# Tying the first experts' matmul groups to turns of the attention on TensorE, and running the fourth block's four full units ahead of their tails

## The chip, the cores and the metric

The kernel runs on one core of one Trainium2 chip. The metric is the device time of one execution in microseconds (us). Before the change the median of 3 runs is 1228.98 us (1228.93 to 1230.21).

## The reference

Three stages follow each other, all in float32. An attention with a threshold (4 batches, 8 heads, 576 rows, head size 64) feeds a first pair of expert matmuls with a squared relu, and that feeds a second pair with a gate (`mish`):

```python
scores = (q @ k.T) / sqrt(64)
scores = where(scores >= max(scores) - tau, scores, -1e9)
attn = exp(scores - max(scores)); attn = attn / (sum(attn) + 1e-9)
x = (attn @ v)                      # to 2304 x 512
r = maximum(x @ w_in, 0); x = (s * r * r + b) @ w_out      # 512 -> 2048 -> 512
h = x @ w2_in; out = (h * tanh(softplus(h))) @ w2_out      # 512 -> 2048 -> 512
```

Float32 precision is reached with pairs of fp32r parts (a high and a low one), so one product takes three matmuls. The second pair is computed with fewer products on sums of quarters, whose weight parts must first be combined.

## The kernel before, in words

**Attention.** Heads go in 16 pairs (four pairs to a batch), and each pair takes nine *turns*; a turn is numbered k = 9 x pair + ti, from 0 to 143. A turn's `scores` (L324) multiplies on TensorE (PE) into the tile S (L340, 4 matmuls, 8 at ti = 4). VectorE (DVE) negates and takes the maximum into ns (L344), ScalarE (ACT) takes the exponential e (L351), DVE masks and sums it (L355), GpSimd (POOL) scales it (L365). From block 0 on S has one buffer (two banks of PSUM), so the next S waits for the L344 before it. Seven turns later (LAG) `weights_t` (L371) transposes a column of e on PE into T (L377 to L386), ACT copies it to te (L388), and a turn after that `product` (L391) multiplies with v into pv (L399). At a pair's last product `split_x` (L407) writes the pair's x with ACT and DVE (L412, L413) and stores a tail of 64 columns to DRAM. Twice in each pair `prep_qk` (L296) makes the next pair's q and k.

**First experts.** `moe1(b)` (L482) treats one batch, called a block: 32 *groups* of 12 matmuls each (`group`, L499, matmuls on L503), 16 into h (`layer1`) and 16 into y (`layer2`). It needs the block's four x, that is x of pair 4b + 3. Each unit's weights w are loaded by the SP queue (L496) into a ring of five slots (for block 0 they are split in place, L63 to L72). ACT makes relu, square and so on of h (L516 to L519), POOL subtracts (L520; DVE in block 3), DVE adds up y (L533). Block 3 runs after the attention, and has beside each full unit (512 columns) a *tail* unit of 256 columns from the tile xt, with the last 64 columns of all four batches.

**Combined weights.** `combine` (L88) makes the second experts' weight parts: raw loads crawi and crawo (L84), then ACT (L98), DVE (L99 to L111, L138), ACT (L136), and stores to wsi and wso (L140) on the SP queue. A step's result tiles share three slots, its intermediate tile has one. The first 12 of 16 steps must be done before the attention's pools are closed; the last four of those 12 are the tiles afo and chlo numbered 0 to 3. Only then is xt placed in that memory and loaded (L848, L849).

**The order.** The program is written by generators that take turns by a running count, attention with higher priority, and a scheduler sets each engine's order from the written order, the priorities and a model of time. Each engine, and the SP queue, then works its instructions off in that order:

```python
if a_on and (not m_on or (a_done - 5000.0) / a_left <= m_done / m_left):
    with tc.high_priority(offset=200):
        c = next(att, None)
else:
    c = next(mo, None)
```

Block 3 takes its units in the order of the list ORDER (L879): part 0 of layer 1 (two full units, two tails), part 1 (two full units, two tails), and so on.

Of the kernel before, what the change touches and what calls it, by code (L numbers as in the profile page):

```python
# [19 lines left out]
class Fused:  # L20
    def __init__(self, tc, q, k, v, tau, w_in, w_out, s, b, w2_in, w2_out, out):
        self.tc, self.nc = tc, tc.nc
        self.q, self.k, self.v, self.tau = q, k, v, tau
        self.s, self.b, self.out = s, b, out
        self.w_in, self.w_out, self.w2_in, self.w2_out = (w.bitcast(I32) for w in (w_in, w_out, w2_in, w2_out))
        self.B, self.H, self.S, self.D = q.shape
        self.NP = self.H // 2
        self.x, self.w1, self.w1s, self.wf, self.g, self.yc, self.ycd, self.es, self.raws = {}, {}, {}, {}, {}, {}, {}, {}, {}
        self.nd = self.n_s = self.n_acc = self.combined = 0
        self.m3 = self.hl = None  # L30


    def consts(self, pool):
# [290 lines left out]
    def scores(self, pr, ti):  # L324
        nc = self.nc
        Q, KH, KL, E4 = self.sets[pr % 2]
        if ti == 0:
            self.st = self.at.tile([P, 5, 9], F32, tag="stat", name=f"st{pr}", bufs=2)
        st = self.st
        nm, nthr, sm, u, rinv = (st[:, i, :] for i in range(5))  # L330
        hs = [0] if ti < 4 else [1] if ti > 4 else [0, 1]
        cols = slice(512, 640) if ti == 4 else slice((ti % 5) * 128, (ti % 5) * 128 + 128)
        S = self.s_tile(f"S{pr}_{ti}")
        for hf in range(2):
            ks = slice(hf * 288, hf * 288 + 288)
            so = S[:, hf * HB:hf * HB + 288]
            terms = [(h, K[h]) for h in hs for K in (KH, KL)]
            for i, (h, kt) in enumerate(terms):
                c0 = ti * 128 + 64 * h if ti <= 4 else 64 + ti * 128
                nc.tensor.matmul(so, Q[:, c0:c0 + 128], kt[:, ks], start=(i == 0), stop=(i == len(terms) - 1))  # L340
        ns = self.at.tile([P, 576], F32, tag="ns", name=f"ns{pr}_{ti}", bufs=2)
        sv = S.rearrange("p (h n) -> p h n", h=2)[:, :, :288]
        c1 = slice(ti, ti + 1)
        nc.vector.tensor_scalar(ns.rearrange("p (h n) -> p h n", h=2), sv, -0.125, 3.0e38,  # L344
                                op0=ALU.mult, op1=ALU.min, accum_out=nm[:, c1])
        nc.vector.tensor_scalar(nthr[:, c1], nm[:, c1], self.tau_c, None, op0=ALU.add)

        if ti < 4:
            self.es[pr, ti, "pair"] = self.at.tile([P, 1152], F32, tag="e", name=f"e{pr}_{ti}", bufs=8)
        e = E4[:, 64:640] if ti == 4 else self.es[pr, ti % 5, "pair"][:, 0 if ti < 4 else 576:][:, :576]  # L350
        nc.scalar.activation(e, ns, AF.Exp, bias=nm[:, c1], scale=-1.0)  # L351
        self.es[pr, ti] = e

        def finish():
            nc.vector.scalar_tensor_tensor(e, ns, nthr[:, c1], e, op0=ALU.is_le, op1=ALU.mult, accum_out=sm[:, c1])  # L355
            if ti not in (1, 4, 8):
                return
            g = slice({1: 0, 4: 2, 8: 5}[ti], ti + 1)
            nc.vector.tensor_scalar(rinv[:, g], sm[:, g], 1.0e-9, None, op0=ALU.add)
            nc.vector.reciprocal(rinv[:, g], rinv[:, g])  # L360

            nc.vector.tensor_scalar(u[:, g], sm[:, g], 0.5, 1.0 / self.S, op0=ALU.is_lt, op1=ALU.mult)
            for j in range(g.start, g.stop):
                t = self.es[pr, j]
                nc.gpsimd.tensor_scalar(t, t, rinv[:, j:j + 1], u[:, j:j + 1], op0=ALU.mult, op1=ALU.add)  # L365

        return finish
# [3 lines left out]
    def weights_t(self, pr, ci):  # L371
        nc = self.nc
        T = self.tp.tile([P, 1024], F32, tag="T", name=f"T{pr}_{ci}")
        E4 = self.sets[pr % 2][3]
        o = ci * 128
        for i in range(4):
            nc.tensor.transpose(T[:, i * 128:i * 128 + 128], self.es[pr, i, "pair"][:, o:o + 128], self.ident)  # L377
        if ci != 4:
            h = 0 if ci < 4 else 1

            c0 = 64 + o - 576 * h
            nc.tensor.transpose(T[:, 512:640], E4[:, c0:c0 + 128], (self.ident, self.swap)[h])  # L382
        else:

            nc.tensor.matmul(T[:, 512:576], E4[:, 0:128], self.ident[:, HALVES[1]], start=True, stop=False)
            nc.tensor.matmul(T[:, 512:576], E4[:, 576:704], self.ident[:, HALVES[0]], start=False, stop=True)  # L386
        te = self.at.tile([P, 576], F32, tag="te", name=f"te{pr}_{ci}", bufs=6)
        nc.scalar.copy(te, T[:, :576])  # L388
        return te

    def product(self, pr, c, tes, first, last):  # L391
# [28 lines left out]
    def attention(self):  # L420
# [2 lines left out]

        nc = self.nc
        N = 9 * self.B * self.NP
        LAG = 7
        for n in "kq":
            self.load_raw(0, n)
        nc.sync.dma_start(self.tau_c, self.tau.partition_broadcast(P))
# [9 lines left out]
        for k in range(N + LAG + 2):  # L439
            pr, ti = divmod(k, 9)  # L440
# [15 lines left out]
            if 0 <= j < N:  # L456
                prj, ci = divmod(j, 9)
                tnew = self.weights_t(prj, ci)
                yield 550
            if todo:  # L460
                tp, tc, te = todo
                tes[tc] = te
                if tc == 4:
                    self.product(tp, 4, (te, te), True, False)
                    yield 490
                elif tc > 4:
                    self.product(tp, tc - 5, (tes[tc - 5], te), False, tc == 8)
                    yield 970
                if tc == 8:
                    self.split_x(tp)  # L470
                    self.load_raw(tp + 2, "v")
            todo = (prj, ci, tnew) if 0 <= j < N else None


# [6 lines left out]

    def moe1(self, b):  # L482

        nc = self.nc
        full = "", [(self.x[4 * b + p][:, 0, :512], self.x[4 * b + p][:, 1, :512]) for p in range(4)], self.gp, 512, b
        runs = [full + (dict(),)]
        if b == 3:
# [10 lines left out]

        def group(acc, w, rhs, n):  # L499
            i = 0  # L500
            for c in range(4):
                for wl, xl in ((0, 0), (0, 1), (1, 0)):
                    nc.tensor.matmul(acc[:, :n], w[:, wl, c], rhs[c][xl], start=(i == 0), stop=(i == 11))  # L503
                    i += 1
                    if i in ((3, 6, 9) if n == 512 else (6,)):
                        yield 680

        def layer1(qf, part):
            ws = {fc: unit(0, qf, fc) for fc in (2 * part, 2 * part + 1)}
            for s, xs, pool, n, _, gs in runs:  # L510
                for fc, w in ws.items():
                    gh, gl = gs[qf, fc] = [pool.tile([P, n], F32R, tag=t, name=f"{t}{s}{b}_{qf}_{fc}", bufs=5 if s else 6) for t in ("gh", "gl")]
                    acc = self.acc(f"h{s}{b}_{qf}_{fc}")
# [21 lines left out]
                    if qf == 3:  # L535
                        nc.sync.dma_start(self.yd[dst, e // 2][:, e % 2], ye)

        for layer, qf, part in ORDER:
            yield from (layer1, layer2)[layer](qf, part)


    def y_combos(self, sb, direct):
# [326 lines left out]


EARLY = 12
HALVES = [slice(0, 64), slice(64, 128)]

N2 = 384
# [48 lines left out]
```

## Time and profile before

| what | value |
|---|---|
| median of 3 runs | 1228.98 us |
| the profiled execution | 1232.59 us, of which the span is 1230.7 us |
| PE matmul busy / weight load (PEld) | 93% / 78% of the span |
| DVE, ACT, POOL busy | 64%, 52%, 20% |
| mean granted TensorE clock | 0.96 |

The profile shows one execution. Times count from the span's start; "<-" after an idle time names what ended it; SPq is the DMA-issuing queue of SP. The clock is given as a share of full speed; it has two levels, 1 (2.4 GHz) and 0.5 (1.2 GHz). On DVE each turn shows two records at L344, the pass over S and a read of its accumulator.

### The profile page before, as it was taken

To read this page: it belongs to the slowest core of one execution; us is meant where nothing else is said; L and a number is where in the kernel's file an instruction comes from. 1 tells how busy PE (TensorE), PEld (TensorE's weight loads), DVE (VectorE), ACT (ScalarE), POOL (GpSimd) and SP (SyncE) were. 2 spreads that over 40 slices of the span, in tenths; PEclk is the share of its full clock that TensorE was granted. 3 is DMA by queue.
4 is the path that set the end of the run, shared out by engine and by line. 5 is a ranking of instruction groups with operands and counts; after the bars stand their busy time and mean duration, and the time that the engine had idled before them with its cause. 6 is when DMAs were issued, how large, how long until landed. Compare 5 with 4: busy or idle time off the path is not lost.

```text
span 1230.7 us, 18932 instructions
## 1 busy us (share of the span) xinstructions
PE 1139.8 (93%) x6796; PEld 956.4 (78%) x6796; DVE 784.9 (64%) x1682; ACT 642.5 (52%) x1061; POOL 243.0 (20%) x234
## 2 busy tenths in 40 slices
PE   7997999989999999899996729999999999999998
PEld 6765766666768777587875318888999999999998
DVE  6978684778724576765548753573479456934683
ACT  4665867464666554586644537763345234523351
POOL 3443432224232221342312200320000000000000
PEclk9998999889999999799997769999999999999999
DMA  6576466556874868678654665894799899998774
GB/s 149 118 184 187 111 218 207 179 180 210 274 209 148 261 227 230 200 247 241 226 153 178 227 232 161 335 384 157 273 357 384 322 392 362 358 328 295 272 252 144
DMA packets 145966, 294.39 MB, mean 239 GB/s; under 512 B 55184, under 2 KB 83344, under 8 KB 137552
## 3 DMA queue, kind: packets, MB, share of 16 engines
q1 hardware_dynamic: 138640, 288.75, 70.4%
q10 hardware_dynamic: 7232, 4.43, 1.4%
q8 instruction: 54, 0.88, 0.3%
q14 instruction: 40, 0.33, 0.1%
HBM read 202.64 MB, written 67.37 MB: 219 GB/s over the span
## 4 chain that ended last, share of the span: by engine, by line
PE 77%; DVE 8%; DMA 5%; issue 3%; POOL 3%; ACT 2%; SPq 1%; ACTq 0%; DVEq 0%; POOLq 0%
PE o L727 14%; PE h L503 13%; PE y L503 12%; PE pv L399 7%; PE qY L593 6%; PE S L340 5%; PE qV L593 4%; PE qX L593 4%; PE T L377 4%; POOL e L365 3%; PE yt L503 2%; PE ht L503 2%; DVE e L355 2%; DVE ns L344 1%; PE T L382 1%
## 5 line engine op out<-in xcount | busy, mean ns | idle before, releaser
L365 POOL TENSOR_SCALAR e<-e,st 128x576 f32<-128x576 f32 x128 | 135.7, 1072 | 245.4 <-DVE st L360 202.3
L727 PE MATMUL o<-wo,hl 128*128 128x256 f32 x1512 | 179.6, 279 | 0.0
L727 PEld LDWEIGHTS o<-wo,hl 128*128 128x128 f32 x1512 | 179.2, 188 | 0.0
L344 DVE TENSOR_SCALAR_CACHE_REDUCE ns<-S 128x576 f32<-128x576 f32 x144 | 107.9, 753 | 102.8 <-PE S L340 101.2
L503 PE MATMUL h<-x,w 128*128 128x512 f32 x576 | 145.8, 402 | 2.7 <-DVE x L413 2.7
L388 ACT COPY te<-T 128x576 f32<-128x576 f32 x144 | 91.7, 637 | 99.4 <-PE T L382 86.6
L377 PE MATMUL T<-ident,e 128*128 128x128 f32 x576 | 107.6, 291 | 30.8 <-ACT te L388 15.8
L355 DVE SCALAR_TENSOR_TENSOR e<-ns,st,e 128x576 f32<-128x576 f32 x128 | 113.2, 889 | 27.1 <-ACT e L351 25.9
L351 ACT ACTIVATE e<-ns,st 128x576 f32<-128x576 f32 x128 | 98.8, 777 | 60.5 <-DVE ns L344 55.0
L503 PEld LDWEIGHTS h<-x,w 128*128 128x128 f32 x576 | 107.5, 192 | 28.9 <-DVE x L413 3.2
L503 PE MATMUL y<-gh,w 128*128 128x512 f32 x384 | 126.3, 397 | 0.6 <-ACT gh L519 0.5
L340 PE MATMUL S<-KH,Q 128*128 128x288 f32 x320 | 101.9, 334 | 23.9 <-DVE ns L344 20.0
L377 PEld LDWEIGHTS T<-ident,e 128*128 128x128 f32 x576 | 73.1, 147 | 64.9 <-ACT te L388 23.8
L399 PE MATMUL pv<-te,rawv 128*64 128x288 f32 x640 | 122.6, 429 | 0.0
L520 POOL TENSOR_TENSOR gl<-r,gh 128x512 fp32r<-128x512 f32 x48 | 65.0, 1356 | 209.6 <-ACT gh L519 169.4
L340 PEld LDWEIGHTS S<-KH,Q 128*128 128x128 f32 x320 | 64.0, 200 | 44.1 <-DVE ns L344 27.0
L340 PE MATMUL S<-KL,Q 128*128 128x288 f32 x320 | 93.1, 306 | 0.0
L593 PE MATMUL qY<-yc,wi 128*128 128x384 f32 x432 | 87.6, 338 | 1.9 <-DVE g L616 1.9
L503 PEld LDWEIGHTS y<-gh,w 128*128 128x128 f32 x384 | 71.8, 188 | 19.3 <-issue 2.2
L593 PEld LDWEIGHTS qY<-yc,wi 128*128 128x128 f32 x432 | 76.3, 187 | 2.9 <-DVE g L616 2.9
L503 PE MATMUL y<-gl,w 128*128 128x512 f32 x192 | 76.3, 398 | 0.0
L645 DVE TENSOR_TENSOR hl<-g,hl 128x768 fp32r<-128x768 f32 x60 | 56.4, 954 | 20.8 <-ACT hl L709 20.7
(152 smaller groups left out, 2013.2 us busy)
## 6 DMA issues: line engine op xcount, KB each, us to landing
w<-w SPq DMA_DIRECT2D x96, 512.0 KB, 4.6
wo<-wso SPq DMA_DIRECT2D x42, 1024.0 KB, 7.2
wi<-wsi SPq DMA_DIRECT2D x23, 1024.0 KB, 8.1
wi<-wsi SPq DMA_DIRECT2D x25, 768.0 KB, 7.6
w<-wp SPq DMA_DIRECT2D x32, 512.0 KB, 3.4
wsi<-chli SPq DMA_DIRECT2D x24, 512.0 KB, 4.3
wso<-chlo SPq DMA_DIRECT2D x24, 512.0 KB, 5.4
ycd<-yp SPq DMA_DIRECT2D x14, 768.0 KB, 8.4
```

The source lines that it names most:

```text
L340: nc.tensor.matmul(so, Q[:, c0:c0 + 128], kt[:, ks], start=(i == 0), stop=(i == len(terms) - 1))
L344: nc.vector.tensor_scalar(ns.rearrange("p (h n) -> p h n", h=2), sv, -0.125, 3.0e38, op0=ALU.mult, op1=ALU.min, accum_out=nm[:, c1])
L351: nc.scalar.activation(e, ns, AF.Exp, bias=nm[:, c1], scale=-1.0)
L355: nc.vector.scalar_tensor_tensor(e, ns, nthr[:, c1], e, op0=ALU.is_le, op1=ALU.mult, accum_out=sm[:, c1])
L365: nc.gpsimd.tensor_scalar(t, t, rinv[:, j:j + 1], u[:, j:j + 1], op0=ALU.mult, op1=ALU.add)
L377: nc.tensor.transpose(T[:, i * 128:i * 128 + 128], self.es[pr, i, "pair"][:, o:o + 128], self.ident)
L388: nc.scalar.copy(te, T[:, :576])
L399: return self.nc.tensor.matmul(self.pv[HALVES[h], hf * HB:hf * HB + 288], v[:, h, c, :], tes[h][:, hf * 288:hf * 288 + 288], start=first, ...
L503: nc.tensor.matmul(acc[:, :n], w[:, wl, c], rhs[c][xl], start=(i == 0), stop=(i == 11))
L520: (nc.vector if b == 3 else nc.gpsimd).tensor_tensor(gl, r, gh.bitcast(F32), op=ALU.subtract)
L593: self.nc.tensor.matmul(acc, a, b, start=(first and i == 0), stop=(i == n - 1), skip_group_check=True)
L727: nc.tensor.matmul(bank[p][t], hl[:, gl, j, ts], w[:, 2 * (q % 2) + j, wl], start=(old is None and q + j + k == 0), stop=(q + j + k == 6), ...
```

## The change

Each turn of the attention keeps the last PE instruction of its scores (from turn 144 on, of its transposes) in a list `turns`. In blocks 0 to 2 the first and the seventh matmul of each group of 12 are queued on PE behind one of these turns: group g (1 to 96 over the three blocks) and half i/12 behind turn 44 + int((g - 1 + i/12) x 36/32), at most the last one. Eight groups so take nine turns, which is 32 groups to four pairs. The link only sets PE's order; it adds no semaphore wait. In block 3 both parts of the first layer-1 entry run as one: four full units, then their four tails.

```diff
+                self.turn = nc.tensor.matmul(so, Q[:, c0:c0 + 128], kt[:, ks], start=(i == 0), stop=(i == len(terms) - 1))
...
+        if 9 * pr + ci + LAG >= 9 * self.B * self.NP:
+            self.turn = turn
...
+            self.turns.append(self.turn.ins)
             todo = (prj, ci, tnew) if 0 <= j < N else None
...
         def group(acc, w, rhs, n):
             i = 0
+            self.groups += 1
             for c in range(4):
                 for wl, xl in ((0, 0), (0, 1), (1, 0)):
-                    nc.tensor.matmul(acc[:, :n], w[:, wl, c], rhs[c][xl], start=(i == 0), stop=(i == 11))
+                    if b < 3 and i % 6 == 0:
+                        turn = self.turns[min(FIRST + int((self.groups - 1 + i / 12) * 36 / 32), len(self.turns) - 1)]
+                        with tc.issue_after(turn):
+                            nc.tensor.matmul(acc[:, :n], w[:, wl, c], rhs[c][xl], start=(i == 0), stop=(i == 11))
+                    else:
+                        nc.tensor.matmul(acc[:, :n], w[:, wl, c], rhs[c][xl], start=(i == 0), stop=(i == 11))
...
-        def layer1(qf, part):
-            ws = {fc: unit(0, qf, fc) for fc in (2 * part, 2 * part + 1)}
-            for s, xs, pool, n, _, gs in runs:
+        def layer1(qf, *parts):
+            held = {}
+            for (s, xs, pool, n, _, gs), part in [(r, p) for r in runs for p in parts]:
+                if not s:
+                    held[part] = {fc: unit(0, qf, fc) for fc in (2 * part, 2 * part + 1)}
+                ws = held[part]
...
-        for layer, qf, part in ORDER:
-            yield from (layer1, layer2)[layer](qf, part)
+        order = ORDER if b < 3 else [(0, 0, 0, 1)] + ORDER[2:]
+        for layer, *key in order:
+            yield from (layer1, layer2)[layer](*key)
...
+LAG = 7
+FIRST = 44
```

The built programs show where the instructions went. In the listings a row is one instruction or a run of equal ones; the line numbers of the changed program are its own.

First place: PE at turns 134 to 136 (the tile S of pair 14's turn 8 and pair 15's turns 0 and 1; T are transposes; h and y are groups of the first experts). Before:

```order
L340 MATMUL S_8_5880<-KH_126,Q_123 128x288
L340 MATMUL S_8_5880<-KL_128,Q_123 128x288
L340 MATMUL S_8_5880<-KH_126,Q_123 128x288
L340 MATMUL S_8_5880<-KL_128,Q_123 128x288
L340 MATMUL S_0_5912<-KH_133,Q_131 128x288
L340 MATMUL S_0_5912<-KL_135,Q_131 128x288
L340 MATMUL S_0_5912<-KH_133,Q_131 128x288
L340 MATMUL S_0_5912<-KL_135,Q_131 128x288
L340 MATMUL S_1_5957<-KH_133,Q_131 128x288
L340 MATMUL S_1_5957<-KL_135,Q_131 128x288
L340 MATMUL S_1_5957<-KH_133,Q_131 128x288
L340 MATMUL S_1_5957<-KL_135,Q_131 128x288
```

The changed program, about turn 136:

```order
L513 MATMUL y_1_3_6506<-gl_1_3_6239,w_1_1_3_6482 128x512
L513 MATMUL y_1_3_6506<-gh_1_3_6238,w_1_1_3_6482 128x512
L341 MATMUL S_1_5957<-KH_133,Q_131 128x288
L341 MATMUL S_1_5957<-KL_135,Q_131 128x288
L341 MATMUL S_1_5957<-KH_133,Q_131 128x288
L341 MATMUL S_1_5957<-KL_135,Q_131 128x288
L511 MATMUL h_2_2_6529<-x_3671,w_0_2_2_6523 128x512
L513 MATMUL h_2_2_6529<-x_3671,w_0_2_2_6523 128x512 x2
L513 MATMUL h_2_2_6529<-x_4113,w_0_2_2_6523 128x512 x3
L511 MATMUL h_2_2_6529<-x_4552,w_0_2_2_6523 128x512
L513 MATMUL h_2_2_6529<-x_4552,w_0_2_2_6523 128x512 x2
L513 MATMUL h_2_2_6529<-x_4999,w_0_2_2_6523 128x512 x3
```

Three S stood directly behind one another; now a whole group of 12 matmuls of block 2 stands between two of them. Counted over the program, the matmuls of blocks 0 to 2 up to S of turn 84 go from 428 to 417, from there up to S of turn 143 from 724 to 639, and behind it from 0 to 96. Turns with none of them, from turn 45 on, were 49, 51, 59 to 62, 69 to 71, 105 to 113 and 133 to 142; in the changed program they are 60, 61 and 68 to 71.

Second place: the SP queue, at the end of the attention (crawo are raw loads of a combination step, chlo its results, w loads into the ring: w_0_0_1 to w_0_0_3 are block 3's first units, yd stores of block 2's results). Before:

```order
L84 DMA crawo_6556<-in_moe_w_out_dram 128x1024
L84 DMA crawo_6558<-in_moe_w_out_dram 128x1024
L140 DMA wso<-chlo_6612 128x512
L140 DMA wso<-chlo_6560 128x2x512
L140 DMA wso<-chlo_6561 128x2x512
L84 DMA crawo_7041<-in_moe_w_out_dram 128x1024
L84 DMA crawo_7043<-in_moe_w_out_dram 128x1024
L140 DMA wso<-chlo_6625 128x2x512
L84 DMA crawo_6693<-in_moe_w_out_dram 128x1024
L84 DMA crawo_6695<-in_moe_w_out_dram 128x1024
L140 DMA wso<-chlo_6697 128x2x512
```

The changed program:

```order
L500 DMA w_0_0_1_6921<-w_0_0_1_1411 128x1024
L141 DMA wso<-chlo_6561 128x2x512
L549 DMA yd_0_61<-y_0_5598 128x512
L549 DMA yd_0_61<-y_1_5599 128x512
L500 DMA w_0_0_2_6965<-w_0_0_2_1593 128x1024
L141 DMA wso<-chlo_6625 128x2x512
L500 DMA w_0_0_3_6967<-w_0_0_3_1670 128x1024
L85 DMA crawo_6693<-in_moe_w_out_dram 128x1024
L549 DMA yd_1_62<-y_2_5600 128x512
L85 DMA crawo_6695<-in_moe_w_out_dram 128x1024
```

Loads into the ring and stores of block 2's results, which stood well ahead of these steps before, now stand between the steps' own loads and stores.

Third place: PE in block 3 (h full units, ht tails). Before:

```order
L503 MATMUL h_0_1_6946<-x_5416,w_0_0_1_6921 128x512 x3
L503 MATMUL h_0_1_6946<-x_5874,w_0_0_1_6921 128x512 x3
L503 MATMUL h_0_1_6946<-x_6258,w_0_0_1_6921 128x512 x3
L503 MATMUL h_0_1_6946<-x_6477,w_0_0_1_6921 128x512 x3
L503 MATMUL ht_0_0_6967<-xt,w_0_0_0_6919 128x256 x3
L503 MATMUL ht_0_1_6988<-xt,w_0_0_1_6921 128x256 x3
L503 MATMUL h_0_2_7013<-x_5416,w_0_0_2_7007 128x512 x3
```

The changed program:

```order
L513 MATMUL h_0_3_6992<-x_5416,w_0_0_3_6967 128x512 x3
L513 MATMUL h_0_3_6992<-x_5874,w_0_0_3_6967 128x512 x3
L513 MATMUL h_0_3_6992<-x_6258,w_0_0_3_6967 128x512 x3
L513 MATMUL h_0_3_6992<-x_6477,w_0_0_3_6967 128x512 x3
L513 MATMUL ht_0_0_7013<-xt,w_0_0_0_6919 128x256 x3
L513 MATMUL ht_0_1_7038<-xt,w_0_0_1_6921 128x256 x3
```

Two full units (24 matmuls) stood ahead of the first one that reads xt, now four do (48).

## Rows read from the trace of the kernel before

**Rows 1.** The page: the span, and its first part on TensorE.

```profile
span 1230.7 us, 18932 instructions
PE 1139.8 (93%) x6796; PEld 956.4 (78%) x6796; DVE 784.9 (64%) x1682; ACT 642.5 (52%) x1061; POOL 243.0 (20%) x234
```

**Rows 2.** Busy time by stretch: stretch, its length, each engine, PE clock, DMA share, GB/s.

```profile
122.90:348.10 225.20, 209.49 (x1071) 152.63 (x1072) 158.97 (x381) 141.57 (x231) 72.18 (x61) 0.96 0.64 200
348.10:681.70 333.60, 313.60 (x1657) 238.43 (x1655) 201.23 (x499) 189.67 (x305) 95.06 (x87) 0.95 0.67 207
681.70:738.00 56.30, 26.51 (x107) 15.09 (x107) 34.92 (x72) 24.61 (x44) 3.96 (x4) 0.69 0.68 239
```

**Rows 3.** The same stretches, L344 on DVE alone (two records to a turn).

```profile
122.90:348.10 225.20, 30.45 (x80) 0.96 0.64 200
348.10:681.70 333.60, 44.95 (x118) 0.95 0.67 207
```

**Rows 4.** The same stretches, the first experts' matmuls (L503) on PE and PEld.

```profile
122.90:348.10 225.20, 115.87 (x429) 79.63 (x430) 0.96 0.64 200
348.10:681.70 333.60, 181.22 (x724) 131.49 (x723) 0.95 0.67 207
```

**Rows 5.** The chain of waits: start, us, what; runs of matmuls.

```profile
752.08 5.44 PE h L503 x24
...
605.93 0.53 PE S L340 x4
...
610.97 0.44 PE T L377 x4
611.51 1.12 PE pv L399 x8
```

**Rows 6.** Two stretches of nine turns each: L344 on DVE, then L503 on PE, PEld.

```profile
391.60:454.00 62.40, 6.86 (x18) 1.00 0.73 224
535.30:600.80 65.50, 6.86 (x18) 1.00 0.80 253
...
391.60:454.00 62.40, 47.25 (x191) 34.46 (x190) 1.00 0.73 224
535.30:600.80 65.50, 46.70 (x193) 35.15 (x192) 1.00 0.80 253
```

**Rows 7.** Busy time by stretch, where next to no L503 stands.

```profile
487.40:521.80 34.40, 27.86 (x152) 19.39 (x151) 27.26 (x77) 17.99 (x29) 9.44 (x9) 0.80 0.69 203
...
207.30:218.70 11.40, 7.17 (x46) 4.98 (x44) 9.95 (x27) 9.12 (x16) 1.28 (x1) 0.98 0.69 219
261.00:273.40 12.40, 7.76 (x35) 6.25 (x34) 9.69 (x26) 9.01 (x15) 1.27 (x1) 0.72 0.91 278
```

**Rows 8.** Timeline at turns 134 and 135: a combination step and the scores.

```profile
656.97 0.62 ACT L136 CAST chli<-afi 128x512 fp32r<-128x512 f32 x1 [4.62 <-DMA wsi<-chli]
...
659.04 0.61 PE L340 MATMUL S<-KH,Q 128*128 128x288 f32 x1 [4.44 <-DVE ns L344]
```

**Rows 9.** Timeline at the end of the attention and the start of block 3.

```profile
684.51 0.41 DVE L99 TENSOR_SCALAR afo<-crawo 128x512 int32<-128x512 int32 x1
...
710.18 7.06 PE L503 MATMUL h<-x,w 128*128 128x512 f32 x24 [2.69 <-DVE x L413]
...
712.00 0.89 SPq L84 DMA_DIRECT2D crawo<-in_moe_w_out_dram  x2
...
714.99 16.69 SPq L140 DMA_DIRECT2D wso<-chlo  x8
...
734.78 0.57 SPq L848 DMA_DIRECT2D xt<-xtd  x1
...
738.07 1.62 PE L503 MATMUL ht<-xt,w 128*128 128x256 f32 x6 [20.83 <-DMA xt<-x]
```

**Rows 10.** Waits of the SP queue from 600 to 739: total us, times, longest.

```profile
SPq L496 <- PE y L503: 13.4, 6, 4.7
SPq L496 <- PE h L503: 13.1, 4, 5.5
```

More of the change, by code (lines that the diff above doesn't have):

```diff
@@ L29, in __init__ @@
         self.nd = self.n_s = self.n_acc = self.combined = 0
-        self.m3 = self.hl = None
+        self.m3 = self.hl = self.turn = None
+        self.turns, self.groups = [], 0
     def consts(self, pool):
@@ L339, in scores @@
                 c0 = ti * 128 + 64 * h if ti <= 4 else 64 + ti * 128
-                nc.tensor.matmul(so, Q[:, c0:c0 + 128], kt[:, ks], start=(i == 0), stop=(i == len(terms) - 1))
+                self.turn = nc.tensor.matmul(so, Q[:, c0:c0 + 128], kt[:, ks], start=(i == 0), stop=(i == len(terms) - 1))
         ns = self.at.tile([P, 576], F32, tag="ns", name=f"ns{pr}_{ti}", bufs=2)
@@ L373, in weights_t @@
         T = self.tp.tile([P, 1024], F32, tag="T", name=f"T{pr}_{ci}")
+        turn = None
         E4 = self.sets[pr % 2][3]
@@ L376, in weights_t @@
         for i in range(4):
-            nc.tensor.transpose(T[:, i * 128:i * 128 + 128], self.es[pr, i, "pair"][:, o:o + 128], self.ident)
+            turn = nc.tensor.transpose(T[:, i * 128:i * 128 + 128], self.es[pr, i, "pair"][:, o:o + 128], self.ident)
         if ci != 4:
@@ L425, in attention @@
         N = 9 * self.B * self.NP
-        LAG = 7
         for n in "kq":
@@ L482, in moe1 @@
     def moe1(self, b):
-        nc = self.nc
+        nc, tc = self.nc, self.tc
         full = "", [(self.x[4 * b + p][:, 0, :512], self.x[4 * b + p][:, 1, :512]) for p in range(4)], self.gp, 512, b
```

## The prediction

> **What bounds the kernel now.** I read the page's head first: PE is busy 93% of 1230.7 us, every other engine at most 64% [rows 1]. So the end is PE's work plus the time in which PE idles or runs at the lower clock, and I looked for where that is, by stretches cut at turns 44, 84 and 143 and at the first tail matmul [rows 2]. The 225.2 us of turns 44 to 83 hold 225.2 - 209.5 = 15.7 us of idle PE, the 333.6 us of turns 84 to 142 hold 20.0, the 56.3 us up to the first tail 29.8. The granted clock there is 0.96, 0.95 and 0.69: with levels 1 and 0.5, some 18, 33 and 35 us at 1.2 GHz. The rest of the program, 492.7 us behind 738.07, the change hardly touches.
>
> The reader should see three causes. First, L503 stands in lumps: 34.4 us of turns 104 to 113 hold next to none of it, and there PE is busy only 27.9 us at a mean clock of 0.80; the two pieces in block 0 look alike [rows 7]. Second, a turn alone has nothing behind which PE could hide a late S: at 653 a store held up ACT 4.62 us, and PE stood 4.44 us [rows 8]. Third, at the end the fourth block runs 24 matmuls at 710.18 and then waits 20.83 us for xt, which comes behind the last combination step's stores [rows 9].
>
> **The unit prices.** A 128x512 matmul at full clock takes 5.44 / 24 = 0.227 us, so a group 2.72 [rows 5]. A turn's attention work on PE I take from two full pairs inside dense stretches at clock 1.00: 62.4 us with 190 matmuls of L503 leave 62.4 - 43.1 = 19.3 us for 9 turns; 65.5 with 192 leave 22.0 [rows 6]. That is 2.15 and 2.44 a turn; I take the middle, 2.3.
>
> **Turns 44 to 83.** Work: 40 turns [rows 3] x 2.3 = 92.0, 429 matmuls [rows 4] x 0.227 = 97.3; together 189.3 of 225.2 us, so 35.9 are lost. The order of the change still has six turns with no expert matmul here where there were nine, since block 0 also waits for its weights to be split. So I let it recover a third, 12 us (ends: 0, since the gaps stay, and 24, if two thirds go). Eleven matmuls move behind turn 84: 2.5 us. Gain 14.5.
>
> **Turns 84 to 142.** Work before: 59 turns x 2.3 = 135.7, 724 x 0.227 = 164.1; 299.8 of 333.6, 33.8 lost. The 19 turns without L503 have that loss for the most part: the 34.4 us piece alone holds about 10 turns, 23 us of work, and so 11 us of loss [rows 7]. After: 639 x 0.227 = 144.8 and the same 135.7, 280.5. What stays lost: nothing, if 12 matmuls (2.7 us) cover every late S; at most the 20.0 us of idle that were there. Dense turns show none [rows 6], but not every stall is as short as 2.7 us [rows 8], so I take 8. New length 288.5, gain 45.0 (33 to 53). Turn 143 so starts at 681.7 - 14.5 - 45.0 = 622.
>
> **Turn 143 to the first tail matmul.** Two chains end here. PE: 96 matmuls moved here x 0.227 = 21.8, nine transposes of a column and six products, 9 x 0.55 + 6 x 1.12 = 11.7 [rows 5], the waits for te and the last x (2.7 [rows 9], and 2 to 3 us for te by estimate), then four full units, 48 x 0.227 = 10.9: ready 50 us behind turn 143. The combination: its last four steps begin at 684.5, behind turn 143 in both orders, and end with xt at 738.07, 56.4 us behind turn 143 [rows 9]. Nothing of them is removed. So they set the end, and the 21.8 us of moved matmuls lie beside them at no cost; without that cover they would add up to 21.8.
>
> The steps may also get slower. On the SP queue the load of crawo for the last step now stands behind three loads into the ring, and its predecessor's stores behind a fourth. Such a load waits for a matmul group to free a slot: SP waited 26.5 us for that in ten cases, each up to 5.5 [rows 10]. The slots for these come free behind 72, 72, 84 and 96 of the 96 moved matmuls, by the PE sum above about 27, 27, 31 and 38 us behind turn 143; before, that crawo load went out at 712.0, 30 us behind it, and the stores at 715.0, 33 behind. So I add 2.6: first tail at 59 us behind turn 143 (ends: 50, where PE binds, and 68, if all three late turns of the queue add up). It starts at 622 + 59 = 681 instead of 738.07: 57 us of gain so far (14.5 + 45.0 - 2.6).
>
> **Block 3.** 24 more full-unit matmuls are done by then: 5.4 us less behind it [rows 5]. PE still waits about 59 - 50 = 9 us for xt, with the risk of the lower clock as before; I count nothing for that.
>
> **Sum.** 14.5 + 45.0 - 2.6 + 5.4 = 62.3. The profiled execution took 1232.59, 3.6 above the median of the runs; from that median, 1228.98 - 62.3 = **1167 us**. Ends of the terms: 24 + 2.5 + 53 + 6.4 + 5.4 = 91 gives 1138, 2.5 + 33 - 11.6 + 5.4 = 29 gives 1200; they will hardly all fall one way.
>
> **Rivals.**
> - *The queues take over the wait* (0.14). Each of the eight combination steps that the order puts into turns 84 to 142 stores through the same SP queue that loads w, and a held-up ACT or SP stops the turn, and now also the matmuls tied to it. Against: the dense turns had such steps too. Price: 4.4 us [rows 8] each, 35 in place of my 8, and up to 9 more in the tail: 1194 to 1203.
> - *The even order also closes the short pauses* (0.10). The pitches of rows 5 make a pair 40 x 0.133 + 46 x 0.11 + 40 x 0.14 = 16 us, about 17 with its 12 small transposes, against the 20.7 I charge. Half of the 3.7, over 11 pairs, is 20 us more: 1147. The Trainium skill, Perfetto Trace Analysis, section Identifying the Most-Contended Engine, says that matmul busy time misjudges how near PE is to its limit and that the busy share of weight loads shows it better. The trace agrees that there is room: 93% against 78% [rows 1].
> - *The combination sets the pace* (0.04). If the 12 steps ran at their own rate, xt would land where it does now, and only 5.4 us would go: 1224. Against: the last four take 50 us, the eight before them had 333.6, so they follow the turns.
> - *The pieces slow the clock* (0.08, the other side). In the dense turns bursts of up to 36 matmuls alternate with attention; now there are pieces of 12, a bit over half of PE's time. If that let the granted clock fall as in rows 7 (0.80, that is 40% of the time at 1.2 GHz), 500 us of turns would have 200 us at half rate instead of about 50: 75 us more, 1167 + 75 = 1242, slower. It decides from about 125 us more at 1.2 GHz on, where 62 us are eaten. Against: nine turns with 190 matmuls, 21 a turn, and 192 ran at 1.00 [rows 6]; for it: no dense row has as few as 11 a turn, and turns 44 to 83, with 429 in 40, had 0.96 [rows 2, 4]. The Trainium skill, the same page, section Matmul Optimizations, speaks for this rival: the engine scales with its use, so matmuls should run back to back in batches, and this change cuts batches up. By that rule the 14.5 and 45.0 would turn into a loss; the rows at 1.00 show mixed streams at full clock, but none as thin.
>
> That the change does nothing can't be: the orders differ as shown.
>
> **How the numbers follow.** My forecast has 0.61, the rivals 0.14, 0.10, 0.04 and 0.08; 0.03 are left for a stall that I don't see and that takes back all (near 1229). A measurement of this kernel tells about 0.2%, 2.5 us. Faster: 0.61 + 0.14 + 0.10 + 0.04 = 0.89; same 0.02; slower 0.08 and 0.01 of the unseen. The range, 1142 to 1205, holds the forecast's ends as far as they are likely, the first rival whole and half of the second; left out are half of the second, 0.05, the third, the fourth and the unseen, 0.20 in all.
>
> **What would show it.** Right: turn 143 (the last L344) near 622; PE idle in turns 84 to 142 at 8 us or less and the clock there at 0.98 or more; the first ht matmul near 681 with a wait for xt of some 9 us; 485 to 488 us from there to the end. Wrong: a clock under 0.95 in that stretch; waits of S for ns above 20 us in it; waits of h or y for loads of w; a first ht later than 65 us behind turn 143; or turns 44 to 83 as long as before.

## The result, and the profile after

The change makes the kernel faster: 1190.88 us, median of 4 runs (1187.2 to 1192.29), beside 1228.95 (1227.69 to 1230.21); the ratio is 0.9686, 95% interval 0.9661 to 0.971. Forecast were 1167 us. The direction and the range (1142 to 1205) held, the size did not: 38 us came of 62.

The page of the kernel after, its head and the clock by slices; beside [rows 1], the span is 42.1 us shorter and PE does the same 6796 matmuls in 16.7 us less busy time; behind the start the clock dips in one slice, from 683 us on:

```profile
span 1188.6 us, 18905 instructions
PE 1123.1 (94%) x6796; PEld 943.2 (79%) x6796; DVE 788.5 (66%) x1682; ACT 640.6 (54%) x1061; POOL 244.6 (21%) x234
...
PEclk9997999999999999999999969999999999999999
```

The same four stretches as in [rows 2], of the kernel after, cut where DVE starts its pass over S (now L345) of turns 44, 84 and 143, at the first tail matmul, and at the end (columns as there):

```profile
124.12:345.76 221.64, 206.19 (x1060) 148.31 (x1061) 159.77 (x381) 138.41 (x226) 70.54 (x59) 0.98 0.63 199
345.76:631.99 286.23, 282.34 (x1559) 213.69 (x1558) 200.08 (x497) 185.15 (x301) 95.92 (x86) 1.00 0.75 230
631.99:701.79 69.80, 49.62 (x240) 34.99 (x239) 39.32 (x76) 34.44 (x60) 6.59 (x6) 0.90 0.73 256
701.79:1188.60 486.81, 480.36 (x3240) 465.13 (x3240) 288.24 (x434) 210.37 (x364) 19.14 (x16) 0.99 0.83 302
```

Set against before, stretch by stretch: turns 44 to 83 lose 3.6 us, turns 84 to 142 lose 47.4, the stretch from turn 143 to the first tail *grows* by 13.5, and the rest loses 5.8. With 1.2 us that this execution was later at turn 44, that is 1.2 - 3.6 - 47.4 + 13.5 - 5.8 = -42.1, the whole difference of the spans. So one stretch made nearly all the gain, one made next to none of the 14.5 us forecast for it, and one gave a part back. Of the 47.4 us, 85 matmuls that now run behind turn 143 are 19.3 (724 before, 639 by the order after, at 0.227 each); the other 28 are for the most part time in which PE idled (20.0 us before, 3.9 after) or ran at the lower clock.

What PE waits for there, by the view of waits (engine, operand and line waited for; total us, times, longest). Turns 84 to 142 first: four rows, 3.8 us, where the S and T rows of before summed to 18.7. The two longest of before, then the four of after:

```profile
PE S L340 <- DVE ns L344: 12.3, 8, 4.4
PE T L377 <- POOL e L365: 4.9, 6, 1.5
...
PE S L341 <- DVE ns L345: 1.1, 2, 0.9
PE S L341 <- DVE loq L282: 1.0, 1, 1.0
PE S L341 <- DVE lok L282: 0.9, 2, 0.7
PE T L379 <- ACT te L390: 0.8, 2, 0.6
```

Turns 44 to 83: three rows of 13.1 us; PE idles 221.64 - 206.19 = 15.5 us, as much as before.

```profile
PE T L379 <- ACT te L390: 4.8, 5, 1.6
PE T L379 <- POOL e L366: 4.4, 7, 1.0
PE S L341 <- DVE ns L345: 3.9, 5, 1.3
```

And from turn 143 to the end the one long wait of [rows 9] is still there, 19.3 us where it was 20.8:

```profile
PE ht L513 <- DMA xt<-x: 19.3, 1, 19.3
```

### The profile page after: what moved, and what is told of

It reads as the page before. It is cut to its first block, busy times and chain, and to the rows that moved or that the text cites. A ratio compares the mean times of both kernels' runs of the same rounds, so it can differ in the third digit from the quotient of the medians.

```text
span 1188.6 us, 18905 instructions
## 1 busy us (share of the span) xinstructions
PE 1123.1 (94%) x6796; PEld 943.2 (79%) x6796; DVE 788.5 (66%) x1682; ACT 640.6 (54%) x1061; POOL 244.6 (21%) x234
## 4 chain that ended last, share of the span: by engine, by line
PE 70%; DVE 5%; DMA 3%; issue 2%; ACT 1%; POOL 1%; SPq 1%; ACTq 0%; DVEq 0%
PE o L741 15%; PE y L513 10%; PE h L513 10%; PE qY L607 6%; PE pv L403 5%; PE qX L607 4%; PE qV L607 4%; PE S L341 4%; PE T L379 3%; PE yt L513 2%; PE ht L513 2%; PE h L511 1%; PE y L511 1%; DMA w<-w 1%; PE T L384 1%
## 5 line engine op out<-in xcount | busy, mean ns | idle before, releaser
L345 DVE TENSOR_SCALAR_CACHE_REDUCE ns<-S 128x576 f32<-128x576 f32 x144 | 107.8, 752 | 61.0 <-PE S L341 59.4
L513 PE MATMUL h<-x,w 128*128 128x512 f32 x512 | 135.2, 399 | 1.2 <-DMA w<-w 1.1
L379 PE MATMUL T<-ident,e 128*128 128x128 f32 x576 | 101.9, 284 | 20.3 <-ACT te L390 13.1
L341 PE MATMUL S<-KH,Q 128*128 128x288 f32 x320 | 101.9, 335 | 13.6 <-DVE ns L345 7.7
L513 PEld LDWEIGHTS h<-x,w 128*128 128x128 f32 x512 | 95.6, 190 | 24.1 <-issue 3.5
L513 PE MATMUL y<-gh,w 128*128 128x512 f32 x320 | 105.9, 391 | 0.0
L659 DVE TENSOR_TENSOR hl<-g,hl 128x768 fp32r<-128x768 f32 x60 | 56.5, 954 | 20.8 <-ACT hl L723 20.7
L513 PEld LDWEIGHTS y<-gh,w 128*128 128x128 f32 x320 | 60.0, 188 | 12.9
```

The source lines that it names most:

```text
L341: self.turn = nc.tensor.matmul(so, Q[:, c0:c0 + 128], kt[:, ks], start=(i == 0), stop=(i == len(terms) - 1))
L379: turn = nc.tensor.transpose(T[:, i * 128:i * 128 + 128], self.es[pr, i, "pair"][:, o:o + 128], self.ident)
```

## The experiments

Twelve kernels ran, each in four to nine executions beside the kernel before on the same chip. The table gives their medians and, of one profiled execution each, the lengths of the four stretches, cut as above. Rows of "windows" in the fences below have the columns of [rows 2].

| kernel | median us | turns 44-83 | turns 84-142 | turn 143 to first tail | to the end |
|---|---|---|---|---|---|
| before | 1228.95 | 225.3 | 333.6 | 56.3 | 492.6 |
| the change | 1190.88 | 221.6 | 286.2 | 69.8 | 486.8 |
| e1 gates only | 1194.81 | 228.0 | 285.7 | 67.1 | 491.3 |
| e2 four units only | 1225.28 | 222.8 | 332.1 | 57.0 | 487.3 |
| e3 no gates in block 0 | 1188.45 | 223.6 | 283.6 | 69.8 | 485.9 |
| e4 last four steps earlier | 1176.35 | 220.9 | 296.2 | 40.4 | 492.4 |
| e5 three steps moved behind xt | 1166.84 | 221.1 | 286.1 | 50.0 | 484.1 |
| e6 splits closer | 1176.90 | 216.6 | 278.8 | 70.0 | 487.6 |
| e7 denser groups | 1203.38 | 221.5 | 315.3 | 55.3 | 486.1 |
| e8 e4 with tails first | 1177.18 | 222.1 | 297.0 | 38.2 | 495.1 |
| e9 e5 and e6 | 1153.80 | 216.2 | 278.6 | 49.9 | 484.4 |
| e10 e9, splits closer still | 1149.51 | 212.6 | 278.3 | 49.9 | 482.6 |
| e11 e9 without gates | 1202.25 | 229.8 | 324.5 | 23.5 | 498.1 |
| e12 eight ring loads on GpSimd's queue | 1190.79 | 220.4 | 285.8 | 71.4 | 486.8 |

My first theory was that the gates give the gain of turns 84 to 142, and that the second part of the change takes back what it gives: its two more units put two more relu chains on ACT and DVE ahead of the last combination step, so xt comes later by as much as is hidden. The rival was that the ring loads, which the gates move ahead of the combination's transfers on the SP queue, make the chain late. The first four runs take the parts apart.

**e1, the gates alone.**

```diff
-        order = ORDER if b < 3 else [(0, 0, 0, 1)] + ORDER[2:]
+        order = ORDER
```

> The change's first part alone: the first experts' groups follow given turns in all four blocks, but the fourth block's four tails come first in their pairs, as before. Theory (the gating gives the gain; the four full units that the second part sets ahead of the tails put two more units' relu chains on ScalarE and VectorE ahead of the last combination step, and so delay xt by about what they hide): turns 84 to 142 take 286 us as in the change, turn 143 runs near 632, the first ht some 62 to 65 us after it (694 to 697 instead of 702), and the run is within 0.3% of the change, 1187 to 1193 us. Rival (the ring loads that now stand ahead of the combination's stores on SP's queue make the chain late, and the second part is worth its 5.4 us): first ht still 70 us after turn 143, and the run 4 to 6 us slower than the change, 1195 to 1197 us.

Measured 1194.81 us (1190.73 to 1197.2), ratio to before 0.9719 (0.9697 to 0.9742). The last two stretches:

```profile
637.01:704.10 67.09, 44.22 (x217) 30.52 (x215) 39.14 (x74) 30.12 (x52) 6.37 (x6) 0.87 0.75 266
704.10:1195.40 491.30, 485.47 (x3264) 469.36 (x3264) 290.17 (x436) 214.53 (x372) 19.39 (x16) 0.99 0.81 299
```

The first tail is 67.1 us behind turn 143, between both expectations, and the run is 3.9 us slower than the change, at the rival's edge. So my theory of the second part was wrong in size: its two units delay xt by 69.8 - 67.1 = 2.7 us and save 491.3 - 486.8 = 4.5 behind it. The other 67.1 - 56.3 = 10.8 us of the late xt come with the gates. (Each length is of one execution. The change, e3, e6 and e12, which hardly differ here, gave 69.8 to 71.4, so 2.7 us is little more than that spread.) (Turn 143 stood at 637.01 here because turns 44 to 83 took 228.0; this profiled execution was the slowest of the four.)

**e2, the four units alone.**

```diff
-                    if b < 3 and i % 6 == 0:
+                    if b < 0 and i % 6 == 0:
```

> The change's second part alone: the first experts' groups follow the attention as before, the fourth block's tails follow four full units. Theory: TensorE does 5.4 us more under its wait for xt, but xt comes 5 to 8 us later (first ht at 743 to 746 us instead of 738), so the run is the same as before within 0.3%, 1226 to 1232 us. Rival: xt still comes at 738 us and the run is 4 to 6 us faster than before, 1223 to 1225 us.

Measured 1225.28 us (1223.48 to 1231.67, 9 runs), ratio 0.997 (0.9951 to 0.9989).

```profile
677.59:734.60 57.01, 28.49 (x125) 16.57 (x124) 36.76 (x73) 28.55 (x51) 5.17 (x4) 0.77 0.66 236
734.60:1221.90 487.30, 480.24 (x3240) 465.16 (x3240) 287.98 (x434) 210.36 (x364) 19.12 (x16) 0.99 0.82 302
```

xt is late by 57.0 - 56.3 = 0.7 us, and the rest is 5.3 us shorter. That is nearly the rival: the second part is worth some 4 us alone as with the gates, not far from its 5.4 us of moved matmuls.

**e3, no gates in the first block.**

```diff
-                    if b < 3 and i % 6 == 0:
+                    if 0 < b < 3 and i % 6 == 0:
```

> The change, with the gates left out for the first block's groups (turns 44 to 83) and kept for the second and third. Theory (the first block's stretch is bound by work that the gates do not move, so its gate gave only the 2 to 4 us that were measured): turn 84 at 346 to 349 us, turns 84 to 142 in 285 to 288 us, the run 0 to 4 us slower than the change, 1190 to 1195 us. Rival (each block's gate matters alike, and the first block's groups left loose disturb the second's): turns 84 to 142 take over 292 us and the run is over 6 us slower than the change, above 1197 us.

Measured 1188.45 us (1186.6 to 1191.7), ratio 0.9675 (0.9653 to 0.9698): no slower than the change, where 0 to 4 us were expected. Turn 84 stands at 347.29, turns 84 to 142 take 283.6. The gates of block 0 are worth nothing here that these runs can tell; the gain is in blocks 1 and 2.

**e4, the last four combination steps earlier.** The steps are written out by a count of matmul groups; here at 18 where it was 12.

```diff
-                    while n * 256 < (2 + 12 * EARLY) * (i + 128 * (b - 1)):
+                    while self.combined < EARLY and n * 256 < (2 + 18 * EARLY) * (i + 128 * (b - 1)):
```

> The change, with the last four of the twelve steps of the combination that feed the fourth block written out earlier, beside the last turns of the attention (the pace is 18 instead of 12 steps to the stretch; same work). Theory (TensorE waits 19.3 us for xt because these four steps lie behind turn 143 in the order of ScalarE's and VectorE's work): the first ht runs when TensorE is ready, about 50 us after turn 143, and the run is 12 to 19 us faster than the change, 1171 to 1179 us. Rival (ScalarE and VectorE have no room for the steps beside the attention): turns 84 to 142 take 296 us or more instead of 286, and the gain is under 8 us, 1183 us or more.

Measured 1176.35 us (1174.15 to 1181.83), ratio 0.9579 (0.9551 to 0.9607).

```profile
343.42:639.59 296.17, 284.64 (x1572) 216.35 (x1571) 227.05 (x552) 197.61 (x327) 105.27 (x86) 0.99 0.82 260
639.59:680.00 40.41, 39.68 (x189) 27.09 (x188) 7.61 (x16) 11.55 (x18) 5.79 (x6) 1.00 0.49 153
680.00:1172.40 492.40, 486.09 (x3280) 469.99 (x3278) 290.28 (x438) 219.58 (x380) 19.18 (x16) 1.00 0.82 300
```

The wait for xt is gone: PE is busy 39.68 of 40.41 us. The first tail runs even earlier than the 50 us I expected, since the order now puts it behind 189 matmuls instead of 240; what it overtakes is paid behind it (492.4 instead of 486.8). And turns 84 to 142 are 10 us longer, with DVE at 227 us of busy time where it had 200, as the rival had it. 14.5 us of gain are left of 19.3: the four steps do set xt, but their place beside the attention costs 10.

**e5, fewer steps ahead of xt.** Instead of pressing them into the attention, three of the twelve steps go behind xt, into the fourth block.

```diff
-                    while n * 256 < (2 + 12 * EARLY) * (i + 128 * (b - 1)):
+                    while self.combined < EARLY and n * 256 < (2 + 12 * 12) * (i + 128 * (b - 1)):
...
-EARLY = 12
+EARLY = 9
```

> The change, with nine instead of twelve steps of the combination done before xt is placed; the other three run beside the fourth block (the pace beside the attention stays). Theory (TensorE's wait for xt is the time that the last steps take on ScalarE, VectorE and SP behind turn 143, and nothing else holds xt back): one step is left behind turn 143, xt lands before TensorE asks for it, the first ht runs 40 to 50 us after turn 143 instead of 70 with no wait, turns 84 to 142 keep their 286 us, and the run is 15 to 19 us faster than the change, 1171 to 1176 us. Rival (the fourth block has no room for three more steps): the first ht is early, but the stretch from it to the end grows from 487 us to over 497, and the gain is under 8 us, 1183 us or more.

Measured 1166.84 us (1166.1 to 1167.96), ratio 0.9503 (0.9484 to 0.9522), 24.0 us faster than the change.

```profile
345.10:631.15 286.05, 282.31 (x1559) 213.74 (x1558) 199.97 (x497) 185.05 (x301) 95.42 (x86) 1.00 0.75 231
631.15:681.10 49.95, 49.22 (x241) 35.28 (x240) 17.13 (x31) 21.12 (x36) 6.37 (x6) 1.00 0.61 198
681.10:1165.20 484.10, 477.55 (x3241) 462.30 (x3239) 307.00 (x467) 223.47 (x389) 42.16 (x28) 1.00 0.86 320
```

Turns 84 to 142 keep their 286 us, PE runs through to the first tail, and the fourth block takes the three steps without growing: 484.1 us. There the steps' low parts are subtracted on POOL (busy 42.2 us instead of 19.1), not on DVE. The gain is more than the 15 to 19 us of the theory, in part by 2.7 us behind the first tail (see the last section).

**e6, the first block's weight splits closer together.** This asks why turns 44 to 83 gained next to nothing.

```diff
-                if i % 4 == 0:
+                if i % 3 == 0:
                     next(w1, None)
```

> The change, with the first block's weight splits written closer together (one more piece of them after every third instead of every fourth quarter of a group). By the order every turn from 45 on then has matmuls of the first experts between its scores and the next (six turns had none in the change), and 432 instead of 417 of them stand ahead of turn 84. Theory (turns 44 to 83 gained only 2 to 4 us because the first block's groups wait for their split weights, so the gates could not fill the turns there): turns 44 to 83 take 210 to 215 us instead of 221.6, with TensorE's idle time in them down from 15.5 to under 9 us, and the run is 6 to 12 us faster than the change, 1179 to 1185 us. Rival (the stretch is bound by VectorE and GpSimd, which make the splits and the attention's e alike): turns 44 to 83 stay at 219 us or more and the run is within 4 us of the change.

Measured 1176.90 us (1176.47 to 1178.01), ratio 0.9587 (0.9565 to 0.9609): 14.0 us faster than the change. The first two stretches, and what PE still waits for in the first:

```profile
121.76:338.32 216.56, 210.14 (x1088) 151.57 (x1089) 162.30 (x382) 143.87 (x236) 75.85 (x62) 0.98 0.69 213
338.32:617.08 278.76, 274.39 (x1531) 209.39 (x1530) 200.22 (x496) 179.58 (x291) 93.00 (x84) 1.00 0.75 229
...
PE T L379 <- POOL e L366: 4.4, 6, 1.2
PE T L379 <- ACT te L390: 1.5, 2, 0.8
```

Idle time of PE falls from 15.5 to 6.4 us and the waits of S for ns disappear, with DVE and ACT no less busy. So the splits were what kept the matmuls from the empty turns, not the engines' load. The stretch is 5.1 us shorter with 28 more PE instructions in it: 15 matmuls of the first experts (3.4 us at 0.227), 8 of products and 5 transposes (1.7 us by the prices of [rows 5]). A second 7.5 us come in the next stretch, which has those 28 and ten ACT instructions less. My bounds for the stretch alone (210 to 215) were a little too good, those for the run (1179 to 1185) not good enough. Where the rest of the stretch goes stays open: at the unit prices it holds about 191 us of work in 216.6.

**e7, all groups ahead of turn 143.** Since e1 laid the late xt to the gates, two causes were left: the 96 matmuls that they leave behind turn 143, or the SP queue. Here no group stays behind it.

```diff
-... int((self.groups - 1 + i / 12) * 36 / 32) ...
+... int((self.groups - 1 + i / 12) * (36 / 32 if self.groups <= 32 else 33 / 32)) ...
```

> The change, with the second and third blocks' groups on 33 instead of 36 turns for each 32, so that all of them stand ahead of turn 143 and none between the last turns' transposes and products. Theory (behind turn 143 ScalarE and VectorE work in order, with the copies of T and the relu chains between the combination's steps, so the 96 matmuls of the second and third experts' groups that the change leaves there hold the combination back by some 11 us): turns 84 to 142 take 305 to 310 us, the first ht runs 55 to 61 us after turn 143 instead of 70, and the run is 5 to 12 us slower than the change, 1196 to 1203 us. Rival (the combination after turn 143 has its own pace, set by its loads and stores): first ht 67 us or more after turn 143, and the run 15 to 20 us slower than the change, 1206 us or more.

Measured 1203.38 us (1202.21 to 1204.97), ratio 0.98 (0.9779 to 0.9822). The window from turn 143 to the first tail, ACT's waits for te and x in it, and DVE's for gh:

```profile
659.17:714.50 55.33, 28.32 (x126) 16.30 (x124) 34.46 (x69) 27.49 (x49) 4.33 (x4) 0.79 0.61 216
...
ACT te L390 <- PE T L384: 3.5, 5, 1.0
...
ACT x L416 <- PE pv L403: 0.2, 1, 0.2
...
DVE gl L533 <- ACT gh L532: 3.5, 1, 3.5
```

The first tail is back at 55.3 us behind turn 143. In the change, the same rows of ACT's and DVE's waits in that window (632 to 702) read:

```profile
DVE gl L533 <- ACT gh L532: 10.2, 2, 6.4
...
ACT te L390 <- PE T L384: 9.1, 6, 2.6
...
ACT x L416 <- PE pv L403: 4.7, 1, 4.7
```

ACT and DVE work their lists off in order. With matmul groups between the last transposes and products on PE, ACT stands 13.8 us at te and x instead of 3.7, and the combination's casts are queued behind. ACT also has more of its own to do there, the groups' relu chains among it: it is busy 34.4 us in this window of the change, 27.5 in e7 and 24.6 in the kernel before. So the groups behind turn 143 are shown to make xt late; which share the waits have and which the added work, no run tells. Turns 84 to 142 grew by 29 us instead of the 19 to 24 expected (101 matmuls are 22.9 us, 8 of products and 5 transposes that now stand ahead of turn 143 are 1.7, and 2.9 are more idle time), so the whole is slower, by 12.5 us.

**e8, e4 with the tails first.**

```diff
-        order = ORDER if b < 3 else [(0, 0, 0, 1)] + ORDER[2:]
+        order = ORDER
```

> The kernel with the last four steps of the combination written out earlier (pace 18), and the fourth block's tails first in their pairs as before the change. Theory (four full units ahead of the tails are worth something only as cover for a wait): without the wait the two orders differ by under 2 us, 1174 to 1178 us. Rival (the order is worth its 4 us by itself): 1179 to 1182 us.

Measured 1177.18 us (1174.1 to 1179.18), ratio 0.9584 (0.9559 to 0.9609), the same as e4. The second part of the change is cover for a wait and nothing else.

**e12, the ring loads off SP's queue.** e7 takes the groups away from behind turn 143 and with them the loads that wait on SP. This run moves only loads: the eight of the last units of block 2 and the first of block 3.

```diff
-            nc.sync.dma_start(w.bitcast(F32), self.w1s[key])
+            (nc.gpsimd if (b, *key[:2]) in ((2, 1, 3), (3, 0, 0)) else nc.sync).dma_start(w.bitcast(F32), self.w1s[key])
```

> The change, with eight loads of weights into the ring (the last four units of the third block, the first four of the fourth) issued on GpSimd's queue instead of SP's, so that the combination's loads and stores behind turn 143 stand behind no load that waits for a slot of the ring; the matmuls' order is kept but for a few rows. Theory (the matmuls behind turn 143 hold the combination back through ScalarE's and VectorE's order): first ht 65 to 71 us after turn 143, the run within 3 us of the change. Rival (SP's waits for ring slots, 9.5 us in that stretch in the change, hold it back): first ht 55 to 61 us after turn 143 and the run 8 to 13 us faster than the change, 1178 to 1183 us. In between, both have a part.

Measured 1190.79 us (1188.77 to 1194.47), ratio 0.9687 (0.9658 to 0.9717): the change's own time. The window from turn 143 to the first tail, then POOL's waits and ACT's in it:

```profile
629.33:700.70 71.37, 49.64 (x241) 35.00 (x239) 40.14 (x76) 34.23 (x60) 10.40 (x13) 0.89 0.71 250
...
POOL w L500 <- PE y L513: 11.0, 3, 4.9
POOL w L500 <- PE h L513: 5.9, 2, 3.1
...
ACT te L390 <- PE T L384: 12.0, 7, 2.8
...
ACT x L416 <- PE pv L403: 4.3, 1, 4.3
```

POOL now does the waiting for ring slots, SP has none of it, and xt comes no earlier. So ring loads that hold up SP's queue were not the cause. What is left is what the groups put on ACT and DVE, beside block 2's stores, which still stand on SP's queue (3.1 us of waits for y and chlo in e12); the rows above point to ACT and DVE, and no run takes that away by itself.

**e9 to e11, both repairs together.** e9 joins the edits of e5 and e6, e10 has the splits after every second quarter (`i % 2`), e11 is e9 without any gate (the edit of e2).

> The change with both: nine steps of the combination ahead of xt, and the first block's weight splits after every third quarter of a group. Theory (the two repairs act at different places, the end of the attention and turns 44 to 83, so their gains of 24.0 and 14.0 us add): turn 143 near 617, the first ht 50 us later, 1150 to 1156 us. Rival (they share ScalarE's and VectorE's time, or the wait for xt comes back): 1160 us or more.

> The same with the splits after every second quarter of a group. Theory (with the splits after every third quarter no turn is without matmuls any more, so the splits are no longer what the groups wait for): within 3 us of the run before it, 1148 to 1158 us. Rival (the splits still come late): another 5 us or more, under 1148 us.

> The kernel with both repairs and without the gates (groups follow the attention as before the change). Theory (the gates are worth what turns 84 to 142 lose to the attention's own pace where no matmuls stand between its scores, whatever is done elsewhere): turns 84 to 142 take 325 to 335 us again, part of it returned behind turn 143, where up to 96 matmuls more or 21 us stood with the gates; 1180 to 1195 us. Rival (the gates repaired mainly what late splits had disturbed): turns 84 to 142 under 310 us and the run under 1172 us.

e9 took 1153.80 us (1152.73 to 1155.46), ratio 0.9385 (0.9359 to 0.9411): the gains of 24.0 and 14.0 add up to within 1 us. e10 took 1149.51 (1146.03 to 1151.6), ratio 0.935 (0.9313 to 0.9386), the fastest of all, 41 us below the change. The intervals of the two overlap, though each of e10's four times is below each of e9's; the 4.3 us between them lie between the theory (within 3) and the rival (5 or more), and stay open. e11 took 1202.25 (1200.2 to 1203.51), ratio 0.9776 (0.9749 to 0.9803), 48.5 us above e9, more than I expected. Its middle stretches:

```profile
354.26:678.72 324.46, 308.81 (x1628) 232.83 (x1627) 199.24 (x500) 179.48 (x293) 91.44 (x84) 0.96 0.66 207
678.72:702.20 23.48, 15.79 (x64) 7.46 (x62) 12.77 (x27) 9.29 (x16) 5.00 (x4) 0.78 0.48 171
```

Turns 84 to 142 are 45.9 us longer than e9's at a clock of 0.96, as the theory had it. What returns behind turn 143 (26.4 us less to the first tail) is paid again: 13.7 us more behind it and 13.6 more in turns 44 to 83. So the gates are worth more in the mended kernel than in the one they were made for: 48.5 us, where e2 against the change gives 34.4. Of the 13.6 us in turns 44 to 83, 34 more matmuls are 7.7; the other 6 suggest that the gates of block 0 are worth something once the splits are there in time, which no run takes alone.

## Why the prediction was right in direction and 24 us off in size

**Turns 84 to 142: right.** Predicted were 288.5 us, measured 286.2. The price of a turn holds: 282.3 us busy less 640 matmuls at 0.227 leaves 137 us, 2.32 for each of 59 turns (2.3 taken). Of the 8 us that I let stay lost, 3.9 did. e3 and e11 show that it is the gates of blocks 1 and 2 that do this.

**Turns 44 to 83: the step that failed first.** I "let it recover a third, 12 us", on the argument that three of nine empty turns would be filled. The ends were 0 and 24; the stretch lost 3.6 us, of which 2.5 are the eleven moved matmuls. The reason for the low end was in the text ("block 0 also waits for its weights to be split"), and I still took the middle. e3 shows that the gates do nothing here, e6 that the splits were in the way. This is 10.9 us of the miss, and nearly all of what turn 143 is late (632 against 622).

**Turn 143 to the first tail: the step that failed second.** "Nothing of them is removed. So they set the end, and the 21.8 us of moved matmuls lie beside them at no cost". They did set the end, but the matmuls were not free: the steps got 13.5 us slower, not 2.6, and the first tail ran at +69.8 where the upper end was 68. Both this place (later than 65) and the one before it (turns 44 to 83 as long as before) stand among the prediction's own signs of being wrong. I looked for a coupling by the ring loads on SP's queue and priced that; e12 shows it to be nothing. The moved matmuls themselves cost, as e7 shows, and by the rows through ACT and DVE, whose in-order lists mix the steps with the copies of T, the cast of x and the relu chains, all of which follow PE: for the groups behind turn 143, e1 against before gives 10.8 us and the change against e7 14.5, and for the two units e1 against the change gives 2.7. The timeline of the change between the last two of the twelve steps shows the second piece (start, us, engine, what, idle time before):

```profile
675.85 0.65 ACT L99 ACTIVATE crawo<-crawo 128x512 f32<-128x512 f32 x1 [2.87 <-DMA crawo<-in_moe_w_out_dram]
...
678.73 0.64 ACT L99 ACTIVATE crawo<-crawo 128x512 f32<-128x512 f32 x1
...
679.97 0.69 DVE L533 TENSOR_TENSOR gl<-r,gh 128x512 fp32r<-128x512 f32 x1 [6.43 <-ACT gh L532]
...
683.67 1.13 ACT L532 CAST gh<-r 128x512 fp32r<-128x512 f32 x2
684.39 1.29 DVE L533 TENSOR_TENSOR gl<-r,gh 128x512 fp32r<-128x512 f32 x2 [3.73 <-ACT gh L532]
684.70 0.64 ACT L530 ACTIVATE r<-r 128x512 f32<-128x512 f32 x1
685.23 0.61 ACT L137 CAST chlo<-afo 128x512 fp32r<-128x512 f32 x1
...
685.87 0.69 DVE L139 TENSOR_TENSOR chlo<-afo,chlo 128x512 fp32r<-128x512 f32 x1 [0.19 <-ACT chlo L137]
...
686.60 0.76 DVE L100 TENSOR_SCALAR afo<-crawo 128x512 int32<-128x512 int32 x2
```

The raw loads of the last step were converted by ACT at 675.85 and 678.73, yet DVE takes them up at 686.60. In DVE's list gl of three of the four full units stands ahead of them, for which it idled 6.43 and 3.73 us, and then the last piece of the step before, whose cast ACT made only at 685.23, among the relu chains of the units; two of the four units the change had put there. PE itself was ready 50.5 us behind turn 143, where the sum had 50.

**Block 3: right.** 5.8 us less against 5.4 predicted.

**The sum.** Two terms are off by 10.9 each; 3.6 us come from working off a profiled execution that stood that far above the median; 1.2 us is turn 44; the good terms give back 2.7. Together that is the 23.9 us between 1167 and 1190.88, to some tenths.

**The rivals.** Queues that take over the wait, and a combination that sets the pace, both fell in turns 84 to 142, where all waits of PE sum to 3.8 us; behind turn 143 the second is half true, since the last steps end last there, at a pace that the groups on PE slow down (e7). The short pauses did not close: 2.32 us a turn, not 17 / 9 = 1.9. And the clock rose instead of falling: 1.00 over 286 us with 640 matmuls in 59 turns, 11 a turn, against 0.95 with lumps [rows 2]. The Trainium skill, Perfetto Trace Analysis, section Matmul Optimizations, asks for matmuls back to back in batches; here the thin even stream had the higher clock, and the stretches with lumps and gaps the lower one, so for this kernel the measurement decides against reading that rule as one for long bursts. PE was busy 282.3 of the 286.2 us there, against 313.6 of 333.6 before.

## What to carry to other kernels

Spread independent matmuls evenly over the steps of a chain on which PE waits, not in lumps; and before crediting it, look for what feeds the spread work (here the splits), since a gate can't fill a turn whose operand is not there. Work moved beside a second chain "at no cost" has to be checked on each engine which that chain shares in order: work that delays PE's last transposes can delay every cast queued behind their copies, and its own chains on those engines come on top. When PE waits at a hand-over, ask first which of the steps ahead of it need to be there at all: moving three of them behind it was worth 24 us, six times the 4 us that more work in front of the wait gave, and more than the 14.5 of doing them earlier.

## What the runs showed of the hardware that was not expected

The wait for xt costs more than its own length. In the kernel after, the granted clock behind the 19.3 us wait, in windows from the first tail on; the last row is e5's first 2 us of tails (PE, PEld and ACT on ht alone):

```profile
701.80:703.80 2.00, 2.00 (x9) 2.00 (x10) 0.00 (x0) 0.00 (x0) 0.00 (x0) 0.50 0.82 223
703.80:705.80 2.00, 2.00 (x9) 1.71 (x8) 0.00 (x0) 0.00 (x0) 0.00 (x0) 0.50 0.58 146
705.80:709.80 4.00, 4.00 (x20) 3.40 (x19) 0.00 (x0) 0.00 (x0) 0.00 (x0) 0.74 0.00 0
709.80:721.80 12.00, 10.92 (x74) 9.79 (x73) 5.25 (x11) 11.43 (x28) 0.00 (x0) 1.00 0.86 307
...
681.10:683.10 2.00, 2.00 (x18) 2.00 (x18) 0.00 (x0) 1.00 0.00 0
```

PE resumes at the level of 1.2 GHz (0.50), with 9 matmuls in 2 us, and reads 1.00, the level of 2.4 GHz, from 709.8 on: by estimate 0.5 x 4 + 0.26 x 4 = 3 us more. e5, where PE did not stop, ran its first tails at 1.00, 18 of them in 2 us, and its last stretch 2.7 us shorter, though it has three combination steps more in it. I had counted "nothing for that". The forecast did not suffer, since the kernel before had the same (0.50 over the first 4 us behind its wait); it is part of what e5 gained.
